# A fused attention and mixture kernel: which queue loads the second batch, and when the later batches' maxima are read

## The chip, the cores and the metric

One core of one Trainium2 chip runs the whole program. The metric is the device time of one launch in microseconds (us), as the median of several runs. The engines are PE (TensorE, matrix products), ACT (ScalarE), DVE (VectorE), POOL (GpSimd) and SP (SyncE, which here issues DMA transfers and nothing else). POOL issues DMA transfers too, between its own arithmetic. Each engine works through a list of its own in order, so an instruction that waits holds up those behind it in that list.

## The reference

```python
q_n, k_n = rmsnorm(q, g_q), rmsnorm(k, g_k)           # x / sqrt(mean(x*x) + 1e-6) * g, over D = 64
scores = (1 / sqrt(64)) * q_n @ k_n.T                 # B, H, S, D = 4, 12, 448, 64
attn = softmax(scores)                                # max taken off, sum + 1e-9
x = (attn @ v).transpose(0, 2, 1, 3).reshape(1792, 768)
h = x @ w_in                                          # 768 x 2048
x = (h * sigmoid(1.702 * h)) @ w_out                  # 2048 x 768
h = x @ w2_in
out = (maximum(h, 0) + alpha * minimum(h, 0)) @ w2_out
```

All inputs are float32, and the output is float32 of 1792 x 768. The weights of the two layers come as 64-bit words.

## The kernel before, in words

**Tiling.** The twelve heads of a batch are handled in NP = 6 pairs, so there are 24 pairs, numbered P = 0 to 23, six to each of the four batches b. A pair's queries and keys are one `qk` tile of four DMA transfers (`load_qk`, L354 to L357, a ring of three tiles), its values one `vr` tile of three (`load_v`, L370, L372, L373). `normalize` (L385) takes one or two pairs: ACT squares (L397), DVE sums them into `ss` (L399), and POOL works out the inverse roots `rs`: L400 and L403, then three rounds of the four operations L407 to L410, 14 in all. Pairs 0 and 1 have a `normalize` each (on 14 columns); later calls take two pairs (28 columns).

**Stages.** Batch 0 runs first, in float32 (`first_pairs`): DVE multiplies with the roots (`qn`, L434), PE transposes, scores, row maxima (`nm`, L506), exponentials on ACT. Beside it the first layer's weights are made: SP loads raw words (L222, into rings of R1I = 5 and R1O = 4 places), ACT and DVE turn them into float32 (`from_words`, L147, L163, L164), DVE takes row maxima (L244), and ACT and DVE split them in two float16 halves (`split_rows`, L179). Batches 1 to 3 run in split float16, with `hl` and `ph` transposed by DMA (L456, L601, L606), while PE interleaves the first layer of the batch before. The second layer follows, from about 600 us on, and keeps PE busy to the end.

**The maxima of v.** A batch's values are scaled by a power of two below their largest magnitude, `av[:, b]`. Batch 0's maximum is taken pair by pair (L446). For batches 1 to 3 `v_scale(b)` (L304) reads the whole batch once more: VN = 8 loads of 128 x 336 float32 into `vst` (L310, two buffers, on POOL's queue), each followed by a DVE reduction into a column of `vcol` (L311), and `v_scales` (L297) then takes the maximum over columns and partitions. `av[:, b]` is first needed when the batch's first pair splits its values into `vs` (`split`, L139 and L140, called at L460).

**What sets the order.** The program is written in one order, and the framework's scheduler, which works with its own estimate of time, writes each engine's list from it. `tc.issue_after(ins)` lets what is in its block be queued on `ins`'s engine only behind `ins`; it binds nothing on other engines. `v_scale(1)` stands in a block behind the last load of the first layer's first weight (L1212, an SP instruction), `v_scale(2)` and `v_scale(3)` behind `moved[P]`, the transposing DMA of a pair's `hl` (L456, L705, an SP instruction too), where P is a batch's next to last pair. The loads L310 are POOL instructions. `load_qk` and `load_v` go to SP's queue for batch 0 and to POOL's for batches 1 to 3 (L353, L369).

Of the kernel before, what the change touches and what calls it, by code (L numbers as in the profile page):

```python
# [56 lines left out]
def attention_moe_kernel(  # L57
# [246 lines left out]
    def v_scale(b):  # L304
        flat = v[b].rearrange("h s d -> (h s d)").rearrange("(p n) -> p n", p=128)
        n = flat.shape[1] // VN
        col = small.tile([128, VN], F32, tag="vcol", name="vcol")
        for i in range(VN):
            t = raw_p.tile([128, n], F32, tag="vst", name="vst")
            nc.gpsimd.dma_start(out=t, in_=flat[:, i * n:(i + 1) * n])  # L310
            nc.vector.tensor_reduce(out=col[:, i:i + 1], in_=t, op=ALU.max, axis=AX, apply_absolute_value=True)  # L311
        v_scales(b, col)

# [28 lines left out]
    def some_rows(src, b, p, first, step=1):  # L342

        return src[b, 2 * p:2 * p + 2, first:first + 64 * step:step].rearrange("h s d -> s h d")

    def load_qk(P):

        if P >= B * NP:
            return
        b, p = divmod(P, NP)  # L350
        qk = raw_p.tile([128, 2, NT2, D], F32, tag="qk", name="qk", bufs=QKB)
        places = qk.rearrange("p h c d -> p h (c d)")
        queue = nc.gpsimd if b else nc.sync  # L353
        queue.dma_start(out=places[:, :, 0:3 * D], in_=main_rows(k, b, p))  # L354
        queue.dma_start(out=places[:, :, 4 * D:], in_=main_rows(q, b, p))
        queue.dma_start(out=qk[0:64, :, 3], in_=some_rows(k, b, p, ST))
        queue.dma_start(out=qk[64:128, :, 3], in_=some_rows(q, b, p, ST))  # L357
        raws[P] = qk

    def load_v(P):  # L360
        if P >= B * NP:
            return
        b, p = divmod(P, NP)
        if b:
            vr = raw_p.tile([128, 2, NV, D], F32, tag="vr", name="vr")
        else:
            firsts[P] = first_tiles(P)
            vr = firsts[P][1]
        queue = nc.gpsimd if b else nc.sync  # L369
        queue.dma_start(out=vr.rearrange("p h c d -> p h (c d)")[:, :, 0:3 * D], in_=main_rows(v, b, p))  # L370
        h = 0 if b else 64
        queue.dma_start(out=vr[h:h + 64, :, 3], in_=some_rows(v, b, p, ST))  # L372
        queue.dma_start(out=vr[64 - h:128 - h, :, 3], in_=some_rows(v, b, p, 0, 3))  # L373
        rawv[P] = vr
# [2 lines left out]
    roots = {}  # L377
    v0 = const.tile([128, NP], F32, name="v0")
    moved = {}

    def side(P):

# [2 lines left out]
    def normalize(*Ps):  # L385

        Ps = [P for P in Ps if P < B * NP]
        if not Ps:
            return
        n = NT2  # L390
        w = 2 * n * len(Ps)
        ss = small.tile([128, 4 * NT2], F32, tag="ss", name="ss")[:, 0:w]
        for t, P in enumerate(Ps):
            flat = raws[P].rearrange("p h c d -> p (h c) d")
            for i in range(2):
                sq = att_p.tile([128, n, D], F32, tag="sq", name="sq", bufs=SQB)
                nc.scalar.activation(out=sq, in_=flat[:, i * n:(i + 1) * n], func=AF.Square, scale=2.0 ** -13)  # L397
                o = (2 * t + i) * n
                nc.vector.tensor_reduce(out=ss[:, o:o + n], in_=sq, op=ALU.add, axis=AX)  # L399
        nc.gpsimd.tensor_scalar(out=ss, in0=ss, scalar1=1e-6 * 2.0 ** -20, scalar2=None, op0=ALU.add)  # L400
        rs = small.tile([128, 4 * NT2], F32, tag="rs", name="rs")[:, 0:w]
        tn = small.tile([128, 4 * NT2], F32, tag="tn", name="tn")[:, 0:w]
        nc.gpsimd.tensor_scalar(  # L403
            out=rs.bitcast(I32), in0=ss.bitcast(I32), scalar1=-0.5, scalar2=RSQRT_SEED, op0=ALU.mult, op1=ALU.add
        )
        for _ in range(3):
            nc.gpsimd.tensor_tensor(out=tn, in0=rs, in1=rs, op=ALU.mult)  # L407
            nc.gpsimd.tensor_tensor(out=tn, in0=tn, in1=ss, op=ALU.mult)
            nc.gpsimd.tensor_scalar(out=tn, in0=tn, scalar1=-0.5, scalar2=1.5, op0=ALU.mult, op1=ALU.add)
            nc.gpsimd.tensor_tensor(out=rs, in0=tn, in1=rs, op=ALU.mult)  # L410
        for t, P in enumerate(Ps):
            eng = side(P)
            ks = raws[P][:, :, 0:4]
            flat = raws[P].rearrange("p h c d -> p (h c) d")
            root = rs[:, 2 * n * t:2 * n * (t + 1)]
            if P < NP:
                roots[P] = root
                continue
            eng.tensor_tensor(out=ks, in0=ks, in1=gs.unsqueeze(1).to_broadcast([128, 2, 4, D]), op=ALU.mult)
            eng.tensor_tensor(out=flat, in0=flat, in1=root.unsqueeze(2).to_broadcast([128, 2 * n, D]), op=ALU.mult)  # L420
# [274 lines left out]
    def other_batches():  # L695
        for i, _ in enumerate(attention(list(range(4 * NP, NU)))):
            P, r = divmod(4 * NP + i, 4)
            if P < B * NP:
# [3 lines left out]
                if r == NORM_AT and P % 2 == 0:  # L702
                    normalize(P + 2, P + 3)
                if r == 2 and P % NP == NP - 2 and P // NP + 1 < B:
                    with tc.issue_after(moved[P].ins):  # L705
                        v_scale(P // NP + 1)
                if r == 3:
                    load_qk(P + 1 + QKB)
# [565 lines left out]
```

## Time and profile before

| | |
|---|---|
| runs | 1175.09, 1175.65, 1180.21 us; median 1175.65 |
| the profiled execution | 1178.25 us, of which the span of the trace is 1176.5 |
| PE busy | 1064.7 us (91% of the span) |
| DVE busy | 818.7 us (70%) |
| ACT busy | 671.9 us (57%) |
| POOL busy | 178.1 us (15%) |
| transfers moved | 158.05 MB, of them 17.11 by POOL's queue |

The shares are means over stages that differ, so the table by stretch, which gives each engine's busy time in a piece of the span, comes first. In a timeline a row gives the start, the duration, the engine, the line and operation, output and input; the bracket at its end is the idle time of the engine just before it and what ended that. An issue of a DMA takes an engine's time, and the transfer goes on after it; "landing" is the time from issue to the data's arrival. The engine name SPq stands for SP's sequencer. "PEclk" is the mean clock granted to TensorE, where 1.00 is 2.4 GHz.

### The profile page before, as it was taken

Reading aid. Unit: us, or ns where it says so; the run is one execution under the profiler, and the core shown is the slowest. Engines: PE = TensorE matmul, PEld = TensorE weight load, DVE = VectorE, ACT = ScalarE, POOL = GpSimd, SP = SyncE. Lnnn points to the kernel's source line nnn. Section 1 sums busy time; section 2 is a strip of 40 time slices with the busy share of each in tenths; the row PEclk is TensorE's granted clock in tenths of the full one; section 3 lists DMA queues with packets and bytes.
Section 4 is the critical chain, followed back from the end, with each engine's and each line's share of the span. In section 5 each row is a group of like instructions: output and inputs, shape, how many; then the busy total and the mean of one; then the engine's idle time right before and its main releaser. Section 6 shows DMA issues by size and latency. Waiting matters only on the chain.

```text
span 1176.5 us, 18337 instructions
## 1 busy us (share of the span) xinstructions
PE 1064.7 (91%) x6755; PEld 586.5 (50%) x6755; DVE 818.7 (70%) x1445; ACT 671.9 (57%) x1348; POOL 178.1 (15%) x350
## 2 busy tenths in 40 slices
PE   1468898679889999999999999999999999999998
PEld 0234456554344445555455455544444477666664
DVE  5979899887776876567651958499987322978351
ACT  3658676687776786668842645266545323645220
POOL 5331002667333323201000000000000000000000
PEclk9679799879999999999999999999999999999999
DMA  8863544477898677566563911465633323353011
GB/s 266 245 209 91 162 139 115 93 146 144 158 182 122 134 139 131 118 117 122 94 132 94 328 45 52 143 221 188 215 110 114 136 76 120 99 177 101 32 33 29
DMA packets 233130, 158.05 MB, mean 134 GB/s; under 512 B 166704, under 2 KB 211888, under 8 KB 233040
## 3 DMA queue, kind: packets, MB, share of 16 engines
q1 hardware_dynamic: 226128, 139.77, 46.0%
q0 software_dynamic: 6912, 17.11, 6.0%
q8 instruction: 53, 0.87, 0.3%
q14 instruction: 37, 0.30, 0.1%
HBM read 92.22 MB, written 25.69 MB: 100 GB/s over the span
## 4 chain that ended last, share of the span: by engine, by line
PE 38%; DVE 21%; DMA 14%; ACT 13%; issue 8%; POOL 5%; SPq 1%; ACTq 0%; DVEq 0%; POOLq 0%
PE op L1058 16%; PE h L898 10%; PE yp L796 5%; ACT pr L525 4%; DMA qk<-in_q_dram 4%; DVE nm L506 3%; PE hp L773 3%; PE hp L726 2%; DVE ph L594 2%; ACT ph L567 2%; DMA g<-in_moe_w_out_dram 2%; DMA yr<-y_dram 1%; DMA t<-hl 1%; DMA w2raw<-in_moe_w_in_dram 1%; DMA g<-in_moe_w_in_dram 1%
## 5 line engine op out<-in xcount | busy, mean ns | idle before, releaser
L796 PE MATMUL yp<-g,w1o 128*128 128x448 f16 x1152 | 226.1, 354 | 0.0
L898 PE MATMUL h<-x,w2i 128*128 128x512 f16 (+1 forms) x1152 | 218.9, 353 | 3.7 <-DVE pos L904 2.9
L773 PE MATMUL hp<-x,w1i 128*128 128x448 f16 x864 | 170.1, 354 | 1.4 <-DVE t L782 1.4
L898 PEld LDWEIGHTS <-w2i 128*128 128x128 f16 x1152 | 112.5, 98 | 109.2 <-issue 4.5
L796 PEld LDWEIGHTS <-w1o 128*128 128x128 f16 x1152 | 109.7, 98 | 108.1 <-issue 8.7
L773 PEld LDWEIGHTS <-w1i 128*128 128x128 f16 x864 | 82.4, 98 | 84.1 <-issue 10.1
L594 DVE SCALAR_TENSOR_TENSOR ph<-pr,sm,ph 128x448 f16<-128x448 f32 x126 | 88.4, 731 | 20.6 <-ACT ph L567 20.5
L506 DVE TENSOR_REDUCE nm<-sp 128x2 f32<-128x896 f32 x96 | 92.3, 961 | 3.0 <-PE sp L501 3.0
L525 ACT ACTIVATE pr<-sp,nm,c_s 128x448 f32<-128x448 f32 x126 | 89.9, 717 | 2.0 <-DVE ph L594 0.6
L903 ACT ACTIVATE pos<-h,sign 128x512 f32<-128x512 f32 (+1 forms) x64 | 40.1, 628 | 86.2 <-PE h L898 80.4
L567 ACT ACTIVATE ph<-pr,sm 128x448 f16<-128x448 f32 x126 | 77.9, 660 | 18.0 <-DVE sm L564 17.9
L1058 PEld LDWEIGHTS <-even 128*128 128x128 f16 x672 | 65.6, 98 | 43.5
L904 DVE SCALAR_TENSOR_TENSOR pos<-h,slope,pos 128x512 f32<-128x512 f32 (+1 forms) x64 | 43.4, 680 | 59.2 <-ACT pos L903 59.2
L726 PE MATMUL hp<-x,w1i 128*128 128x256 f16 (+1 forms) x576 | 66.5, 279 | 11.3 <-DVE t L738 7.8
L501 PE MATMUL sp<-t 64*128 64x448 f16 (+1 forms) x432 | 54.8, 361 | 17.5 <-ACT pr L525 16.3
L726 PEld LDWEIGHTS <-w1i 128*128 128x128 f16 x576 | 56.4, 105 | 22.5 <-issue 17.5
L1058 PEld LDWEIGHTS <-odd 128*128 128x128 f16 x504 | 49.3, 98 | 32.6
L1058 PE MATMUL op<-w2lo,even 128*128 128x384 f16 x384 | 63.4, 326 | 0.0
L140 DVE SCALAR_TENSOR_TENSOR g<-t,ratio_w1o,g 128x448 f16<-128x448 f32 x64 | 44.7, 705 | 18.4 <-ACT g L139 18.0
L622 PE MATMUL xp<-pt,vs 128*64 128x256 f16 (+1 forms) x792 | 47.2, 265 | 8.8 <-DMA pt<-ph 6.7
L139 ACT ACTIVATE g<-t,ratio_w1o 128x448 f16<-128x448 f32 x64 | 42.0, 664 | 20.8 <-DVE t L782 18.6
L508 ACT ACTIVATE nm<-nm,c_s 128x2 f32<-128x2 f32 x72 | 20.8, 289 | 54.7 <-DVE nm L506 54.5
(236 smaller groups left out, 1644.8 us busy)
## 6 DMA issues: line engine op xcount, KB each, us to landing
g<-in_moe_w_in_dram SPq DMA_DIRECT2D x24, 512.0 KB, 5.7
g<-in_moe_w_out_dram SPq DMA_DIRECT2D x32, 384.0 KB, 4.1
w2raw<-in_moe_w_in_dram SPq DMA_DIRECT2D x24, 512.0 KB, 5.6
w2raw<-in_moe_w_out_dram SPq DMA_DIRECT2D x16, 768.0 KB, 6.4
g_dram<-pos SPq DMA_DIRECT2D x48, 256.0 KB, 2.0
gp<-g_dram SPq DMA_DIRECT2D x8, 1024.0 KB, 7.3
odd<-g_dram SPq DMA_DIRECT2D x6, 1024.0 KB, 5.4
y_dram<-y SPq DMA_DIRECT2D x24, 224.0 KB, 3.4
```

Of the source, the lines that this page charges most:

```text
L140: nc.vector.scalar_tensor_tensor(out=dst[1], in0=src, scalar=scale, in1=dst[0], op0=ALU.mult, op1=ALU.subtract)
L501: nc.tensor.matmul(out=sp[:, j, 0:S] if n == 2 else sp[ds, 0, 0:S], lhsT=qt[ds] if n == 2 else qt[ds, 64:128], rhs=kt[ds, 0:S], start=(i = ...
L506: nc.vector.tensor_reduce(out=nm[:, 0:n], in_=sp[:, 0:n, 0:S], op=ALU.max, axis=AX, negate=True)
L525: nc.scalar.activation(out=pr[i], in_=sp[:, i, 0:S], func=AF.Exp, bias=nm[:, i:i + 1], scale=c_s if u >= 4 * NP else 1.0, accum_out=sm[:, ...
L567: nc.scalar.activation(out=ph[:, i, 0:S], in_=pr[i], func=AF.Copy, scale=sm[:, i:i + 1])
L594: nc.vector.scalar_tensor_tensor(out=ph[:, i, S:2 * S], in0=pr[i], scalar=sm[:, i:i + 1], in1=ph[:, i, 0:S], op0=ALU.mult, op1=ALU.subtract)
L622: nc.tensor.matmul(out=xp[64 * j:64 * j + 64, t:t + n], lhsT=vs[ks, j, c], rhs=pt[ks, 7 * j + kc, 0:n] if b else pt[ks, kc, o:o + n], star ...
L726: nc.tensor.matmul(out=ps, lhsT=w1i[:, kk, e, m * 128:(m + 1) * 128], rhs=xs[0, kk][:, f, cols], start=(i == 0), stop=(i == 3 * KD - 1))
L773: nc.tensor.matmul(out=ps, lhsT=w1i[:, kk, e, m * 128:(m + 1) * 128], rhs=x[:, f], start=(n == 0), stop=(n == 3 * KD - 1))
L796: nc.tensor.matmul(out=ps, lhsT=w1o[:, m, e, j * 128:(j + 1) * 128], rhs=g[:, m, f], start=(n == 0), stop=(n == 3 * KF - 1))
L898: nc.tensor.matmul(out=ps, lhsT=w2i[:, kk, e, m * 128:(m + 1) * 128], rhs=x2[kk][:, f], start=(c == 0), stop=(c == 3 * KD - 1))
L1058: nc.tensor.matmul(out=ps, lhsT=ops[:, o, m, f], rhs=rhs[:, e], start=(c == 0), stop=(c == 3 * KH - 1))
```

## The change

Three edits:

- `v_scale(1)` loads its eight `vst` tiles on SP's queue; those of batches 2 and 3 stay on POOL's.
- A new function `loader(P)` picks the queue of a pair's loads: SP for pairs 0 to 7, POOL from pair 8 on. So the loads of pairs 6 and 7 (batch 1's first two, 14 transfers) change to SP. With the eight `vst` loads that is 22 transfers from POOL to SP.
- `normalize` keeps its last POOL instruction, the last L410, in `rooted[Ps[0]]`, and the blocks of `v_scale(2)` and `v_scale(3)` stand behind `rooted[P + 2]` in place of `moved[P]`. That is a POOL instruction, as the loads are: the roots of pairs 12 and 13 for batch 2, of pairs 18 and 19 for batch 3.

```diff
-            nc.gpsimd.dma_start(out=t, in_=flat[:, i * n:(i + 1) * n])
+            (nc.sync if b == 1 else nc.gpsimd).dma_start(out=t, in_=flat[:, i * n:(i + 1) * n])
...
+    def loader(P):
+
+        return nc.gpsimd if P >= NP + 2 else nc.sync
+
...
-        queue = nc.gpsimd if b else nc.sync
+        queue = loader(P)
...
+    rooted = {}
...
-            nc.gpsimd.tensor_tensor(out=rs, in0=tn, in1=rs, op=ALU.mult)
+            rooted[Ps[0]] = nc.gpsimd.tensor_tensor(out=rs, in0=tn, in1=rs, op=ALU.mult)
...
-                    with tc.issue_after(moved[P].ins):
+                    with tc.issue_after(rooted[P + 2].ins):
                         v_scale(P // NP + 1)
```

The line `queue = ...` occurs twice, in `load_qk` and in `load_v`. Line numbers behind L347 grow by 4 in the changed kernel, behind L369 too, and by 5 behind L383: L354 becomes L358, L370 becomes L374, L410 becomes L415. L310 and L222 keep theirs. No instruction is added or left out; the lists of PE, ACT and DVE hold the same instructions in another order.

**POOL at the start.** The first pairs' roots before, with the first loads of `vst` and of `vr` ahead of them (the `vr` rows are those of pairs 6 and 7):

```order
L370 DMA vr<-in_v_dram 128x2x192
L372 DMA vr<-in_v_dram 64x2x64
L373 DMA vr<-in_v_dram 64x2x64
L310 DMA vst<-in_v_dram 128x336 x2
L400 TENSOR_SCALAR ss<-ss 128x14
L403 TENSOR_SCALAR rs<-ss 128x14
L407 TENSOR_TENSOR tn<-rs 128x14
L408 TENSOR_TENSOR tn<-tn,ss 128x14
L409 TENSOR_SCALAR tn<-tn 128x14
L400 TENSOR_SCALAR ss<-ss 128x14
L410 TENSOR_TENSOR rs<-tn,rs 128x14
L310 DMA vst<-in_v_dram 128x336
```

and now:

```order
masks.py:199 AFFINE_SELECT ident<-ident 128x128
L405 TENSOR_SCALAR ss<-ss 128x14
L408 TENSOR_SCALAR rs<-ss 128x14
L412 TENSOR_TENSOR tn<-rs 128x14
L413 TENSOR_TENSOR tn<-tn,ss 128x14
L414 TENSOR_SCALAR tn<-tn 128x14
L415 TENSOR_TENSOR rs<-tn,rs 128x14
L412 TENSOR_TENSOR tn<-rs 128x14
L413 TENSOR_TENSOR tn<-tn,ss 128x14
L414 TENSOR_SCALAR tn<-tn 128x14
L415 TENSOR_TENSOR rs<-tn,rs 128x14
L412 TENSOR_TENSOR tn<-rs 128x14
```

The first pair's 14 operations now follow one another, and neither `vr` nor `vst` loads stand before them; the second pair's come behind.

**SP around the transfer of a maximum through DRAM** (L127 writes the column `am` out as `line`, L128 reads it back as `row`; `g_143` is the place of the raw weight words). Before:

```order
L357 DMA qk<-in_q_dram 64x2x64
L222 DMA g_143<-in_moe_w_in_dram 128x1024 x5
L127 DMA line_7326<-am 128x1
L128 DMA row<-line_7326 128x128
L222 DMA g_143<-in_moe_w_in_dram 128x1024 x5
L222 DMA g_143<-in_moe_w_out_dram 128x4x192 x31
```

and now:

```order
L222 DMA g_143<-in_moe_w_in_dram 128x1024 x2
L358 DMA qk<-in_k_dram 128x2x192
L359 DMA qk<-in_q_dram 128x2x192
L222 DMA g_143<-in_moe_w_in_dram 128x1024
L360 DMA qk<-in_k_dram 64x2x64
L361 DMA qk<-in_q_dram 64x2x64
L222 DMA g_143<-in_moe_w_in_dram 128x1024 x3
L310 DMA vst<-in_v_dram 128x336 x4
L222 DMA g_143<-in_moe_w_out_dram 128x4x192
L310 DMA vst<-in_v_dram 128x336
L222 DMA g_143<-in_moe_w_out_dram 128x4x192
L310 DMA vst<-in_v_dram 128x336 x3
```

Before, the pair of rows L127, L128 is followed by w_in loads and 31 loads of w_out. Now the rest of the w_in loads has a `qk` tile of pair 6 or 7 between, and the eight `vst` loads of batch 1 stand around the first two loads of w_out.

**POOL behind the roots of pairs 12 and 13.** Before:

```order
L410 TENSOR_TENSOR rs<-tn,rs 128x28
L370 DMA vr<-in_v_dram 128x2x192
L372 DMA vr<-in_v_dram 64x2x64
L373 DMA vr<-in_v_dram 64x2x64
L354 DMA qk<-in_k_dram 128x2x192
L355 DMA qk<-in_q_dram 128x2x192
L356 DMA qk<-in_k_dram 64x2x64
L357 DMA qk<-in_q_dram 64x2x64
L400 TENSOR_SCALAR ss<-ss 128x28
L403 TENSOR_SCALAR rs<-ss 128x28
```

and now:

```order
L415 TENSOR_TENSOR rs<-tn,rs 128x28
L310 DMA vst<-in_v_dram 128x336 x3
L374 DMA vr<-in_v_dram 128x2x192
L376 DMA vr<-in_v_dram 64x2x64
L377 DMA vr<-in_v_dram 64x2x64
L310 DMA vst<-in_v_dram 128x336
L358 DMA qk<-in_k_dram 128x2x192
L359 DMA qk<-in_q_dram 128x2x192
L360 DMA qk<-in_k_dram 64x2x64
L361 DMA qk<-in_q_dram 64x2x64
L310 DMA vst<-in_v_dram 128x336 x3
L405 TENSOR_SCALAR ss<-ss 128x28
```

Behind the last root operation there now stand seven of batch 2's eight `vst` loads among the loads of a later pair's `vr` and `qk`, ahead of the next roots. Batch 3's eight stand in the same way behind the roots of pairs 18 and 19.

## Rows read from the trace of the kernel before

**Rows 1.** Table by stretch; its columns are in the first line of the fence.

```profile
core 0: us, PE busy (x) PEld busy (x) DVE busy (x) ACT busy (x) POOL busy (x), PEclk, DMA share, GB/s
0.00:30.00 30.00, 6.33 (x18) 2.97 (x19) 16.85 (x37) 10.30 (x17) 15.84 (x45) 1.00 0.85 267
30.00:62.00 32.00, 17.19 (x79) 9.45 (x78) 32.00 (x66) 21.91 (x43) 10.62 (x24) 0.68 0.83 255
62.00:77.00 15.00, 11.65 (x59) 5.51 (x58) 8.32 (x20) 7.00 (x17) 6.71 (x17) 0.77 0.60 142
77.00:120.00 43.00, 31.79 (x192) 18.25 (x194) 42.88 (x77) 33.73 (x69) 8.28 (x14) 0.84 0.44 136
...
180.00:215.00 35.00, 29.18 (x292) 24.93 (x293) 31.80 (x72) 21.19 (x43) 10.33 (x24) 1.00 0.28 74
...
285.00:345.00 60.00, 51.91 (x403) 26.48 (x401) 46.04 (x77) 44.56 (x109) 25.73 (x49) 1.00 0.86 164
...
435.00:600.00 165.00, 165.00 (x1148) 83.58 (x1143) 106.68 (x183) 117.71 (x273) 26.08 (x55) 1.00 0.61 117
600.00:1176.50 576.50, 564.74 (x3217) 308.12 (x3215) 353.69 (x556) 247.55 (x382) 0.00 (x0) 1.00 0.38 122
sum 1176.50, PE 1064.71 PEld 586.47 DVE 818.66 ACT 671.92 POOL 178.09; mean PE 88.73 PEld 48.87 DVE 68.22 ACT 55.99 POOL 14.84
```

**Rows 2.** Timeline of POOL, 10 to 17 us: start, duration, what it does, idle before.

```profile
10.81 0.26 POOL L400 TENSOR_SCALAR ss<-ss 128x14 f32<-128x14 f32 x1 [3.61 <-DVE ss L399]
...
12.04 0.21 POOL L409 TENSOR_SCALAR tn<-tn 128x14 f32<-128x14 f32 x1
16.00 0.26 POOL L400 TENSOR_SCALAR ss<-ss 128x14 f32<-128x14 f32 x1 [3.75 <-DVE ss L399]
```

**Rows 3.** Timeline of DVE, first 62 us.

```profile
22.36 1.09 DVE L434 TENSOR_TENSOR qn<-qk,rs 128x896 f32<-128x896 f32 x1 [2.04 <-POOL rs L410]
```

**Rows 4.** Timeline of SP, issues only.

```profile
5.45 0.61 SPq L373 DMA_DIRECT2D w1o<-in_v_dram  x1
...
62.68 0.33 SPq L127 DMA_DIRECT2D line<-am  x1
71.24 0.33 SPq L128 DMA_DIRECT2D row<-line  x1
71.74 9.80 SPq L222 DMA_DIRECT2D g<-in_moe_w_in_dram  x5
94.37 90.11 SPq L222 DMA_DIRECT2D g<-in_moe_w_out_dram  x31
```

**Rows 5.** Timeline of DVE, 62 to 130 us.

```profile
72.39 0.50 DVE L311 TENSOR_REDUCE vcol<-vst 128x1 f32<-128x336 f32 x1 [3.57 <-DMA vst<-in_v_dram]
...
76.33 0.28 DVE L133 TENSOR_REDUCE a<-row 128x1 f32<-128x128 f32 x1 [3.11 <-DMA row<-line]
```

**Rows 6.** Chain of waits, 285 to 345 us: start, duration, what.

```profile
306.64 0.73 POOL qk L354
...
308.69 6.37 DMA qk<-in_q_dram
```

**Rows 7.** Tile view of `vst`: line, engine, count, ns min/median/max, first to last start.

```profile
L310 POOL DMA_DIRECT2D vst<-in_v_dram x24: 536/556/792, 6.1 to 111.3; - x24
L311 DVE TENSOR_REDUCE vcol<-vst x24: 481/492/503, 15.8 to 114.6; 128x1 f32<-128x336 f32 x24
...
DMA to landing us min/median/max: 2.4/4.0/7.4
```

**Rows 8.** Timeline of DVE once more, around 99 us.

```profile
98.86 0.49 DVE L311 TENSOR_REDUCE vcol<-vst 128x1 f32<-128x336 f32 x1
99.27 0.14 DVE L104 TENSOR_SCALAR rm_w1i<-rm_w1i 128x1 f32<-128x1 f32 x1
```

**Rows 9.** Timeline of POOL around 295 us.

```profile
295.19 0.24 POOL L410 TENSOR_TENSOR rs<-tn,rs 128x28 f32<-128x28 f32 x1
```

**Rows 10.** Timeline of DVE, 283 to 345 us.

```profile
340.17 0.75 DVE L140 SCALAR_TENSOR_TENSOR vs<-vr,av,vs 128x512 f16<-128x512 f32 x1 [0.50 <-ACT vs L139]
```

More of the change, by code (lines that the diff above doesn't have):

```diff
@@ L368, in load_v @@
             vr = firsts[P][1]
-        queue = nc.gpsimd if b else nc.sync
+        queue = loader(P)
         queue.dma_start(out=vr.rearrange("p h c d -> p h (c d)")[:, :, 0:3 * D], in_=main_rows(v, b, p))
```

## The prediction

> **What bounds the kernel now.** The table by stretch comes first [rows 1]. From 435 to 600 us PE is busy for 165.00 of 165.00 us, and from 600 to the end for 564.74 of 576.50. Over the span PE is idle 1176.50 - 1064.71 = 111.8 us, 11.8 of them behind 600 and none from 435 to 600, so 100.0 us of idle PE lie ahead of 435. Only from these can a change of order take time; what it adds behind 435 shows only if it makes PE wait.
>
> In the early part DVE is the bound: 32.00 of 32.00 us from 30 to 62, 42.88 of 43.00 from 77 to 120, and still 31.80 of 35.00 from 180 to 215 [rows 1]. A DVE instruction taken out there moves what stands behind it forward by its own time. From 285 to 345 none of the engines is full (PE 51.91, DVE 46.04 of 60.00), and the DMA share is 0.86 [rows 1]: there the chain of waits goes through POOL's issue of a pair's `qk` and a landing of 6.37 us [rows 6].
>
> Three places stand out in the timelines. POOL begins the first pair's roots at 10.81, gets as far as L409 at 12.04, and goes on only behind the second pair's L400, which starts at 16.00 after 3.75 us of idling for `ss` [rows 2]. DVE starts the first `qn` (L434) at 22.36, 2.04 us idle for those roots [rows 3]. And DVE idles 3.57 us for a `vst` load and 3.11 us for `row`, while SP, having issued `line` at 62.68, sends `row` only at 71.24 [rows 4, 5].
>
> **The change part by part.** The sum stands against the profiled execution of 1178.25 us (span 1176.5, and 1.75 around it), which is 2.60 above the median of the runs, 1175.65; each difference is then taken from the median.
>
> A. *Sixteen reductions leave the first 215 us.* All 24 loads of `vst` go out between 6.1 and 111.3 us, and their reductions run from 15.8 to 114.6 [rows 7]. Now only batch 1's eight stay there; those of batches 2 and 3 come behind the roots of pairs 12 and 18. A reduction starts at 98.86 and the next instruction at 99.27, so it takes 0.41 us of DVE's line [rows 8]: 16 x 0.41 = 6.6. The two maxima over columns that follow later are left out of the sum. DVE is the bound there, so I take all: **-6.6** (bounds 0 and -6.6).
>
> B. *The first pair's roots run without a break.* Four operations, 10.81 to 12.04, are 0.31 each [rows 2], so 14 take 4.3 and end at 15.1, and `qn` could start 22.36 - 15.1 = 7.2 earlier. But DVE did other needed work in between, and only the 2.04 it idled are sure [rows 3]. **-2.0** (bounds 0 and -7.2).
>
> C. *The wait for `row`.* SP's place for L127 and L128 among the w_in loads stays, so their 71.24 - 62.68 = 8.6 stay too [rows 4]. The 3.57 for `vst` go, but without other work DVE would wait as long for `row`. DVE's new list has five `qn` ahead of the reduction of `row`, where four were; one is 1.09 long [rows 3]. **-1.1** (bounds 0 and -3.1, the whole second wait [rows 5]).
>
> D. *SP gets 22 issues more, POOL 22 fewer.* POOL's are no price: it is busy 15.84 of 30.00 at the start and 8.28 of 43.00 from 77 to 120 [rows 1]. On SP four `qk` issues now stand between w_in loads behind `row`, 0.61 each [rows 4]: 2.4. The eight `vst` loads stand around the first two w_out loads. They have two buffers, so they go in four rounds of issue, landing and reduction, 0.56 + 4.0 + 0.49 = 5.05 each [rows 7], 20.2 together; SP had 94.37 - (71.74 + 9.80) = 12.8 with nothing to issue in that place [rows 4]. What is over, 7.4, is the upper bound, the lower 0. I take the four issues, **+2.4**.
>
> What stands in SP's line costs more than its issue here: 31 w_out loads are drawn out over 90.11 us, 2.9 a load [rows 4], since each waits for a free place. The Trainium skill (DMA: Bandwidth & Descriptors, section "Issuing engines are not separate DMA queues") says that transfers started by any engine run on the same 16 DMA engines and interleave, so that the choice of issuer only saves issue time, usually small. By that D would be about 0 and the total 2.4 lower, 1169.3; the rows on waiting issues speak against so small a view of it.
>
> E. *Batch 2's loads now lie around 295 to 325 us.* Their block follows the last L410 of pairs 12 and 13, at 295.19 [rows 9]. `av` of batch 2 is first needed by pair 12's `vs`, whose DVE part runs at 340.17 [rows 10], 45 us later, so the maximum itself is in time. What can be late is what is queued behind the loads. On POOL four of them stand ahead of the next `qk` loads, which before went out at 306.64 [rows 6]: two rounds, 10.1, fit in the 306.64 - 295.43 = 11.2 between. On DVE the eight reductions are new, 8 x 0.41 = 3.3, in a stretch where DVE is busy 46.04 of 60.00 and holds up the chain. If every round trip lay open, E would be 4 x 5.05 = 20.2. Since the rounds fit the gap on POOL, I take the reductions alone, **+3.3** (bounds 0 and +20.2).
>
> F. *Batch 3's loads* follow the roots of pairs 18 and 19, in the stretch with PE full and DVE busy 106.68 of 165.00 [rows 1]: 58.3 us of DVE idle cover 3.3 of reductions. **0** (upper bound one round, 5.05, if that cover fails at the one place).
>
> Sum: -6.6 - 2.0 - 1.1 + 2.4 + 3.3 + 0 = **-4.0**, so 1174.25 for an execution like the profiled one, and **1171.7** for the median.
>
> **The rivals.** About 0.5%, 5.9 us, is what a measurement of this kernel can tell from no change: faster is below 1169.8, slower above 1181.5.
>
> R1, *the late loads are hidden and the start gives more.* B is taken halfway to its bound (-4.6), D and E are 0: -6.6 - 4.6 - 1.1 = -12.3, 1163.4. For it: the gap on POOL and the 45 us before the maximum is needed; and at the start the DMA share is 0.85 [rows 1], with 22 transfers fewer crowding the first landings. Against: DVE's work in the break was needed anyway.
>
> R2, *DVE's freed time turns into waits for words.* The reductions leave, but the weights still arrive as they did, with a DMA share of 0.83 from 30 to 62 [rows 1], and DVE waits for them: 0, 1175.7. Against: DVE showed no idle time at all in that stretch.
>
> R3, *slower: the round trips of batch 2's loads lie open.* The place is DVE's line around 295 to 325: a reduction waits there for its landing with the row maxima and `hl` behind it, and POOL's next load for that reduction, with `qk` behind it. Price: 20.2 in place of 3.3, so -7.3 + 20.2 = +12.9, 1188.6. It decides from E = 13.2 on (-7.3 + 13.2 = 5.9). For it: landings of 6.37 are on the chain there [rows 6], and DMA is at 0.86. Against: POOL's gap of 11.2.
>
> R4, *it doesn't do what it says*: the framework could order the loads early again. POOL's new list shows them behind the roots, so 1175.7 is nearly excluded.
>
> R5, *POOL's loads land late because DVE is busy.* With every landing at the longest seen, 7.4, a round is 0.56 + 7.4 + 0.49 = 8.45 [rows 7], four are 33.8: -7.3 + 33.8 = +26.5, 1202.2. Against: DVE was full from 30 to 62 with such loads in flight, and of 24 none took over 7.4, half of them 4.0 or less. The Trainium skill (SBUF — State Buffer, section "SBUF: two separate sides") has such a rule: a transfer issued by GpSimd is starved of descriptors while VectorE holds the port they share, in some of its modes. The trace does not show it at work.
>
> **How the numbers follow.** Forecast 0.45, own range 1166.5 to 1175.5 (D and E each some 4 lower or higher); R1 0.22; R2 0.13; R3 0.15; R4 0.02; R5 0.03. Faster: R1 and four ninths of the forecast's case, 0.22 + 0.20 = 0.42. Slower: R3 and R5, 0.18. Within 0.5%: the rest of the forecast's case 0.25, R2 and R4, 0.40. The low end of the range is R1 with B and C at their bounds, -6.6 - 7.2 - 3.1 = -16.9, 1158.8, so 1159. The high end, 1183, is E at 14.7, short of R3's full price; it leaves out R5, two thirds of R3 and the tails.
>
> **What would show it.** Eight `vcol` reductions before 215 us in place of 24. First `qn` near 15 to 20 in place of 22.36 (B). SP's `row` still some 8.6 behind `line` (C). The first w_out load at 94 or later by no more than 7 (D). The last L415 of pairs 12 and 13 near 295.19 - 7.3 = 288, and pair 12's `vs` near 336 (E). DVE waiting for `vst` for under 5 us in all between 285 and 345; over 13 would be R3. PE full from about 431. The prediction is wrong if that last point does not move, or moves by over 12.

## The result, and the profile after

The changed kernel takes 1182.99 us in the median of 22 runs (1176.80 to 1190.82), the kernel before 1175.47 in its 22 (1169.29 to 1180.21). The ratio is 1.0070, 95% interval [1.0054, 1.0087]: slower by some 8 us. Forecast were 1171.7, and 0.18 for slower. The time lies just inside the range that was given (1159 to 1183), on the wrong side of no change. The profiled execution took 1184.22 us, its span is 1182.4, 5.9 more than before.

The table by stretch of the changed kernel, with the columns of [rows 1]:

```profile
core 0: us, PE busy (x) PEld busy (x) DVE busy (x) ACT busy (x) POOL busy (x), PEclk, DMA share, GB/s
0.00:30.00 30.00, 12.77 (x37) 6.00 (x37) 18.56 (x38) 13.42 (x27) 7.79 (x34) 1.00 0.72 227
30.00:62.00 32.00, 16.42 (x69) 8.19 (x69) 29.09 (x62) 20.34 (x39) 10.16 (x28) 1.00 0.86 252
77.00:120.00 43.00, 33.37 (x206) 17.60 (x204) 40.84 (x83) 33.85 (x73) 0.00 (x0) 0.87 0.49 141
285.00:345.00 60.00, 48.01 (x343) 23.61 (x342) 46.66 (x85) 42.04 (x104) 28.19 (x53) 0.91 0.99 183
...
435.00:600.00 165.00, 164.18 (x1144) 83.29 (x1139) 107.48 (x184) 117.66 (x273) 28.26 (x58) 1.00 0.62 120
600.00:1182.40 582.40, 571.40 (x3246) 311.67 (x3244) 356.12 (x561) 250.45 (x389) 0.00 (x0) 1.00 0.38 122
```

DVE is no longer full from 30 to 62 and from 77 to 120, as was meant. From 285 to 345 the DMA share has gone from 0.86 to 0.99 and PE's busy time from 51.91 to 48.01. Behind 435 PE is nearly as full as before (164.18 of 165.00 in place of 165.00).

What the start gained is there. POOL's timeline, the first pair's roots, against [rows 2]:

```profile
9.36 0.26 POOL L405 TENSOR_SCALAR ss<-ss 128x14 f32<-128x14 f32 x1 [8.06 <-DVE ss L404]
...
13.25 0.22 POOL L415 TENSOR_TENSOR rs<-tn,rs 128x14 f32<-128x14 f32 x1
```

They run from 9.36 to 13.47 without a break, and the first `qn` starts at 13.50 in place of 22.36 [rows 3]; the second row is the reduction of `row`, 6.2 us earlier than in [rows 5] with a wait for it as long as before, 3.40 in place of 3.11 (DVE's timeline):

```profile
13.50 1.09 DVE L439 TENSOR_TENSOR qn<-qk,rs 128x896 f32<-128x896 f32 x1 [0.39 <-POOL rs L415]
...
70.12 0.29 DVE L133 TENSOR_REDUCE a<-row 128x1 f32<-128x128 f32 x1 [3.40 <-DMA row<-line]
```

SP's timeline, against [rows 4]: `row` goes out 7.3 us behind `line` (8.6 before), and the first w_out load at 91.19 (94.37 before), though four `vst` loads stand ahead of it. Counted from `line`, which itself comes 5.3 earlier, that load is 33.8 behind, where it was 31.7.

```profile
57.40 0.34 SPq L127 DMA_DIRECT2D line<-am  x1
64.67 0.33 SPq L128 DMA_DIRECT2D row<-line  x1
...
78.49 10.27 SPq L310 DMA_DIRECT2D vst<-in_v_dram  x4
91.19 0.38 SPq L222 DMA_DIRECT2D g<-in_moe_w_out_dram  x1
```

The tile view of `vst`, against [rows 7]: eight loads on SP between 78 and 100 us, sixteen on POOL from 292.8 on; the longest landing is 9.3 in place of 7.4.

```profile
L311 DVE TENSOR_REDUCE vcol<-vst x24: 470/495/504, 87.1 to 430.6; 128x1 f32<-128x336 f32 x24
L310 POOL DMA_DIRECT2D vst<-in_v_dram x16: 537/567/627, 292.8 to 427.5; - x16
L310 SPq DMA_DIRECT2D vst<-in_v_dram x8: 327/375/717, 78.5 to 100.0; - x8
...
DMA to landing us min/median/max: 2.2/3.7/9.3
```

POOL's timeline around 295, against [rows 9]: the last root operation of pairs 12 and 13 comes at 292.13, only 3.1 us earlier than before.

```profile
262.71 0.78 POOL L374 DMA_DIRECT2D vr<-in_v_dram  x1 [3.31 <-DVE vs L140]
...
292.13 0.24 POOL L415 TENSOR_TENSOR rs<-tn,rs 128x28 f32<-128x28 f32 x1
292.76 1.23 POOL L310 DMA_DIRECT2D vst<-in_v_dram  x2 [0.38 <-issue]
```

The chain of waits from 285 to 365 us: it still goes through the landing of a `qk` load, now 9.06 in place of 6.37 [rows 6], and twice in these rows through a transposing DMA.

```profile
297.84 4.04 DMA t<-hl
...
306.52 9.06 DMA qk<-in_q_dram
...
333.54 5.24 DMA t<-hl
```

DVE's timeline: of the eight reductions of batch 2 one waits for its load, for 1.00 us; pair 12's `vs` is at 343.82, 3.7 later than in [rows 10].

```profile
321.77 0.50 DVE L311 TENSOR_REDUCE vcol<-vst 128x1 f32<-128x336 f32 x1 [1.00 <-DMA vst<-in_v_dram]
...
343.82 0.75 DVE L140 SCALAR_TENSOR_TENSOR vs<-vr,av,vs 128x512 f16<-128x512 f32 x1
```

Batch 3's loads do not lie where step F of the prediction had them. In the kernel before, the roots of pairs 18 and 19 end at 402.73, ahead of the stretch from 435 on in which PE is full, and the changed kernel issues batch 3's loads from 405.56 to 428.0 (POOL's timelines, before and after):

```profile
402.49 0.24 POOL L410 TENSOR_TENSOR rs<-tn,rs 128x28 f32<-128x28 f32 x1
```

```profile
405.56 1.19 POOL L310 DMA_DIRECT2D vst<-in_v_dram  x2
```

PE's last wait ahead of 600 us ends at 421.96 in the kernel before (2.26 long) and at 445.72 here (0.73 long; PE's timelines).

Three marks cut the span into four stages: SP's first transpose of `hl`, DVE's part of `vs` of pair 10, and that of pair 18. In the kernel before, and then in the changed one (SP's and DVE's timelines):

```profile
213.68 2.63 SPq L456 DMA_TRANSPOSE t<-hl  x1
302.11 0.73 DVE L140 SCALAR_TENSOR_TENSOR vs<-vr,av,vs 128x512 f16<-128x512 f32 x1
481.09 0.75 DVE L140 SCALAR_TENSOR_TENSOR vs<-vr,av,vs 128x512 f16<-128x512 f32 x1 [1.23 <-ACT vs L139]
```

```profile
206.42 9.65 SPq L461 DMA_TRANSPOSE t<-hl  x2
299.76 0.73 DVE L140 SCALAR_TENSOR_TENSOR vs<-vr,av,vs 128x512 f16<-128x512 f32 x1
485.51 0.75 DVE L140 SCALAR_TENSOR_TENSOR vs<-vr,av,vs 128x512 f16<-128x512 f32 x1 [1.23 <-ACT vs L139]
```

| stage | before | after | difference |
|---|---|---|---|
| 1: start to first `hl` transpose | 213.7 | 206.4 | -7.3 |
| 2: to pair 10's `vs` | 88.4 | 93.3 | +4.9 |
| 3: to pair 18's `vs` | 179.0 | 185.8 | +6.8 |
| 4: to the end | 695.4 | 696.9 | +1.5 |

So in these two executions the early gain came, more than half of it was given back before the first late load was issued (292.76), and the stretch with the late loads lost as much again.

### The profile page after: what moved, and what is told of

The parts are those of the page before. It is cut to its first block, busy times and chain, and to the rows that moved or that the text cites. A ratio compares the mean times of both kernels' runs of the same rounds, so it can differ in the third digit from the quotient of the medians.

```text
span 1182.4 us, 18333 instructions
## 1 busy us (share of the span) xinstructions
PE 1074.1 (91%) x6755; PEld 587.0 (50%) x6755; DVE 823.5 (70%) x1445; ACT 672.8 (57%) x1348; POOL 161.4 (14%) x328
## 4 chain that ended last, share of the span: by engine, by line
PE 37%; DVE 23%; DMA 15%; ACT 13%; issue 7%; POOL 3%; SPq 2%; ACTq 0%; DVEq 0%; POOLq 0%
PE op L1063 16%; PE h L903 7%; PE yp L801 6%; ACT pr L530 4%; DMA qk<-in_q_dram 3%; DVE nm L511 3%; PE hp L778 3%; DVE ph L599 3%; PE hp L731 3%; DMA t<-hl 2%; DMA yr<-y_dram 2%; ACT ph L572 2%; PE xp L627 2%; DVE g L140 1%; DMA g<-in_moe_w_in_dram 1%
## 5 line engine op out<-in xcount | busy, mean ns | idle before, releaser
L801 PE MATMUL yp<-g,w1o 128*128 128x448 f16 x1152 | 229.5, 357 | 2.4 <-DVE t L743 1.9
L599 DVE SCALAR_TENSOR_TENSOR ph<-pr,sm,ph 128x448 f16<-128x448 f32 x126 | 91.2, 750 | 17.4 <-ACT ph L572 17.4
L506 PE MATMUL sp<-t 64*128 64x448 f16 (+1 forms) x432 | 57.2, 369 | 21.9 <-ACT pr L530 15.3
L627 PE MATMUL xp<-pt,vs 128*64 128x256 f16 (+1 forms) x792 | 49.7, 272 | 13.0 <-DMA pt<-ph 8.9
L627 PEld LDWEIGHTS <-vs 128*64 128x64 f16 x792 | 38.9, 114 | 29.6 <-issue 16.7
```

Source lines behind the costliest of these rows:

```text
L506: nc.tensor.matmul(out=sp[:, j, 0:S] if n == 2 else sp[ds, 0, 0:S], lhsT=qt[ds] if n == 2 else qt[ds, 64:128], rhs=kt[ds, 0:S], start=(i = ...
L599: nc.vector.scalar_tensor_tensor(out=ph[:, i, S:2 * S], in0=pr[i], scalar=sm[:, i:i + 1], in1=ph[:, i, 0:S], op0=ALU.mult, op1=ALU.subtract)
L627: nc.tensor.matmul(out=xp[64 * j:64 * j + 64, t:t + n], lhsT=vs[ks, j, c], rhs=pt[ks, 7 * j + kc, 0:n] if b else pt[ks, kc, o:o + n], star ...
L801: nc.tensor.matmul(out=ps, lhsT=w1o[:, m, e, j * 128:(j + 1) * 128], rhs=g[:, m, f], start=(n == 0), stop=(n == 3 * KF - 1))
```

## The experiments

In the pieces of code below, `...` stands for what is left out of a line. Three theories stood at first. **L**: the late loads of batches 2 and 3 cost the time. **Q**: the change of queues does. **O**: the scheduler's lists come out in another order in a stretch that the diff does not name, and that order does. Ratios are to the kernel before, with 95% intervals.

**The two halves of the change.**

```diff
# q_only: the changed kernel with
-                    with tc.issue_after(rooted[P + 2].ins):
+                    with tc.issue_after(moved[P].ins):
# r_only: the changed kernel with
-            (nc.sync if b == 1 else nc.gpsimd).dma_start(out=t, ...)
+            nc.gpsimd.dma_start(out=t, ...)
-        return nc.gpsimd if P >= NP + 2 else nc.sync
+        return nc.gpsimd if P >= NP else nc.sync
```

> Only the queues change: batch 1's vst loads and the loads of pairs 6 and 7 go to SP, the later batches' loads stay unbound as before. Theory L (the late loads of batches 2 and 3 cost the time, in the stretch from 290 to 435 us): within 4 us of the kernel before, 1171 to 1179, since no load is late. Theory Q (the queue change costs it, through SP's longer line): 5 us or more slower than before, 1181 or more. Theory O (the lists of POOL, SP and DVE come out in another order from 215 us on, and that order costs it, whatever caused it): 3 to 5 slower, if this list is like the changed kernel's there.

> Only the late loads: batches 2 and 3 behind the roots, queues as before. Theory L: slower than before by 3 to 10, 1179 to 1186, with PE reaching 435 us later by as much, since 16 reductions fewer early give at most 6.6 and the late loads cost more. Theory Q: no slower than before, 1169 to 1175. Theory O: 3 to 5 slower only if its list from 215 on is like the changed kernel's.

Measured: q_only 1169.14 (0.9934 [0.9909, 0.9959]), r_only 1183.67 (1.0058 [1.0034, 1.0083]). Theory Q falls: the queue part alone is faster than the kernel before, by 6.6 us in the median, and so than the changed one. The late loads alone are slower by about as much as the whole change. In q_only all sixteen loads of batches 2 and 3 go out from 102 to 144 us (tile view of `vst`):

```profile
L310 POOL DMA_DIRECT2D vst<-in_v_dram x16: 536/538/773, 102.4 to 143.8; - x16
L310 SPq DMA_DIRECT2D vst<-in_v_dram x8: 328/375/552, 79.3 to 100.8; - x8
```

**Without the sixteen loads and reductions.**

```diff
     def v_scale(b):
+        if b > 1:
+            v_scales(b, vcols[1])
+            return
```

> The changed kernel without the 16 loads and reductions of batches 2 and 3, which take batch 1's maximum in place of their own. Theory L: 8 to 14 faster than the changed kernel, 1169 to 1175, since the whole of what is late is gone and the early gain stays. Theory Q: still slower than before, 1179 to 1183. Theory O: 3 to 5 of the loss stays, 1177 to 1180.

> The kernel before without the 16 loads and reductions of batches 2 and 3, which take batch 1's maximum in place of their own; queues as before. It prices the sixteen early reductions: 6.6 if DVE's line is the bound there (1168 to 1170), 0 to 2 if other waits take their place (1174 to 1176). Theory L has after_none within 3 of this run, theory Q has after_none 5 or more above it.

Measured: after_none 1176.99 (0.9999 [0.9971, 1.0026]), before_none 1174.69 (0.9989 [0.9962, 1.0015]). The late block costs 0.7% with either choice of queues: after_none to the changed kernel 0.0071, before_none to r_only 0.0069. Yet after_none stands 2 above the range that theory L gave it, and its lists leave the changed kernel's from 112 us on, so a part of the difference may be order. And the sixteen early reductions cost next to nothing: taking them from the kernel before saves 1.3 us by the ratio, at most 4.5 by the interval, where step A had 6.6. Stranger, after_none does strictly less than q_only: it lacks the sixteen loads and reductions, its lists differ from 102 us on otherwise in order alone, and it is 0.65% above it.

**The two halves of the queue part.** l_only takes `loader`, v1_only `nc.sync` for batch 1's `vst`, each put into the kernel before.

> Of the queue part only the loads of pairs 6 and 7 go to SP; all vst loads stay on GpSimd and unbound as before. Theory P (the gain of the queue part, 6.6, comes from GpSimd's line at the start: pairs 6 and 7's v loads stood ahead of the first roots): most of the gain, 1169 to 1172, with the first qn some 5 us earlier than before. Theory V (it comes from the vst loads that no longer stand between the roots): no gain, 1174 to 1178, first qn near 22 as before.

> Of the queue part only batch 1's eight vst loads go to SP, behind the last load of the first weight; the rest as before. Theory V: most of the gain of the queue part, 1168 to 1172, first qn some 5 us or more earlier. Theory P: no gain, 1174 to 1178. If neither of the two halves gains, the gain hangs on both together or on the order of the lists behind 215 us.

Measured: 1174.00 (0.9974 [0.9953, 0.9994]) and 1175.95 (0.9981 [0.9957, 1.0005]). Neither of P and V holds alone: each half gives 0.2 to 0.3% of the whole part's 0.5 to 0.7, v1_only's interval takes in no change, and the two are not told apart. The first `qn` starts at 23.29 in l_only, later than before, and at 16.03 in v1_only (DVE's timelines). So it is the `vst` loads between the roots that held up the first `qn`, as V has it; but l_only gains no less without that, so the time of the first `qn` is not what the gain hangs on.

**Loads or reductions?** Two theories of the late block, T (transfers) and W (DVE's line).

```diff
# after_nored
-            nc.vector.tensor_reduce(...)
+            if b == 1:
+                nc.vector.tensor_reduce(...)
# after_noload, for b > 1
-            t = raw_p.tile([128, n], F32, tag="vst", name="vst")
-            nc.gpsimd.dma_start(out=t, ...)
+            t = w1i[:, 0, 0, 0:2 * n].bitcast(F32)
```

> The changed kernel with the late loads of batches 2 and 3, but without their 16 reductions; their maxima are batch 1's. Theory T (the transfers cost it: 1.38 MB more for each batch in a stretch whose DMA share is 0.86, and longer landings of qk): stays near the changed kernel, 1180 to 1184. Theory W (DVE's reductions and their waits for landings, in order ahead of other work, cost it): falls to the kernel without both, 1175 to 1179.

> The changed kernel without the late loads; the 16 reductions stay, at the same place in DVE's list (behind the scaling of pair 12 and of pair 18), over data that is long in SBUF, and the maxima are batch 1's. Theory T: falls to the kernel without both, 1175 to 1179. Theory W: the work alone is 3.3 a batch and no landing is waited for, so between, 1178 to 1182.

In after_noload `rooted` is also the last scaling with the roots (L433, on DVE) in place of the last root operation, so the reductions stay late: batch 2's eight stand in one piece from 298.8 to 302.2.

Measured: after_nored 1181.33 (1.0037 [1.0010, 1.0064]), after_noload 1175.86 (0.9987 [0.9969, 1.0004]). Sixteen late reductions without loads cost nothing; late loads without reductions do, by about half of the changed kernel's 0.7%. Whether the reductions add the rest when they come with their loads is not told apart: the intervals overlap. From 290 to 345 us, the row of the table by stretch of after_noload and then of the changed kernel (columns as above):

```profile
290.00:345.00 55.00, 48.65 (x339) 23.96 (x338) 41.05 (x80) 40.95 (x99) 18.55 (x40) 0.94 0.76 162
```

```profile
290.00:345.00 55.00, 43.01 (x302) 20.88 (x299) 42.52 (x82) 39.40 (x96) 23.19 (x47) 0.91 0.98 186
```

Without the loads the DMA share is 0.76 in place of 0.98, and PE is busy for 5.6 us more. But the share does not tell the kernels apart. The same row of after_half (half of each late load, below) and of q_only (no late loads at all):

```profile
290.00:345.00 55.00, 48.99 (x365) 24.02 (x363) 43.22 (x84) 42.23 (x105) 24.89 (x49) 0.97 1.01 188
```

```profile
290.00:345.00 55.00, 49.03 (x354) 23.55 (x353) 41.56 (x76) 43.39 (x107) 19.29 (x35) 0.96 0.93 174
```

At 1.01 and 0.93 PE is as busy there as at 0.76. The landings of `qk` tell more: the longest from 290 to 345 us is 9.1 in the changed kernel, 9.4 in r_only and 11.3 in after_sp (tile views of `qk`), and 4.9 to 7.2 in all other kernels. Among these are after_nored (5.9) and after_vr10b (6.1), whose late loads are full too, so the landings do not tell all.

**Fewer bytes, another issuer, other places.** after_half loads 168 of the 336 columns of each late tile, after_t8 8 of them; after_sp puts the late loads on `nc.sync` behind `moved[P]`; late3_only keeps `rooted[P + 2]` for batch 3 alone; after_r6 puts both behind `rooted[NP]`, the roots of pairs 6 and 7.

> The changed kernel with loads of half the width for batches 2 and 3 (their maxima are taken over half of the values): as many loads and reductions, half the bytes. Theory T by bytes: half of what the late loads cost, so 1178 to 1181. If the number of round trips and issues sets it: as the changed kernel, 1181 to 1185.

> The changed kernel with late loads of 8 columns in place of 336 (maxima of batches 2 and 3 over those): as many loads, issues and reductions, 1/42 of the bytes, SP's list word for word that of the changed kernel. Theory T by bytes: ratio to before 0.998 to 1.001, as with no loads at all. If issues and round trips or the order of the lists cost it: 1.004 to 1.007, as the changed kernel.

> The changed kernel with the late loads of batches 2 and 3 on SP's line, behind the transposing DMA of the pair where the block stands. If the transfers themselves cost it, whoever issues them: 1180 to 1186, as the changed kernel. If GpSimd's line costs it (loads ahead of qk issues and of roots): 3 us or more faster than the changed kernel, 1175 to 1180. If SP's transposes wait behind loads that wait for a buffer: 1187 or more.

> The changed kernel, but only batch 3's loads are late; batch 2's are unbound and early, as in the kernel with the queue part alone (1169). If batch 2's late loads cost it: 1169 to 1173. If batch 3's cost as much: 1174 to 1178. If any late block brings the unfavourable list from 110 to 300 us: 1177 or more.

> The changed kernel with the loads of batches 2 and 3 queued behind the roots of pairs 6 and 7, near 200 us, where the DMA share was 0.28 to 0.32, in place of behind those of pairs 12 and 18. Theory T: free of the cost from 300 us on; that stretch (pair 10's vs to pair 18's vs) falls from 185.8 to 173 to 180, and the ratio to 0.995 to 1.001, unless GpSimd's line, where these loads now stand between qk loads, gives it back from 210 to 300.

| kernel | late loads | median | ratio | interval |
|---|---|---|---|---|
| after_noload | none | 1175.86 | 0.9987 | [0.9969, 1.0004] |
| after_t8 | 16, 8 columns | 1177.02 | 1.0024 | [0.9999, 1.0049] |
| after_half | 16, 168 columns | 1180.54 | 1.0007 | [0.9986, 1.0029] |
| changed kernel | 16, 336 columns | 1182.99 | 1.0070 | [1.0054, 1.0087] |
| after_sp | 16, 336 columns, on SP | 1186.67 | 1.0061 | [1.0033, 1.0089] |
| late3_only | 8, 336 columns | 1180.73 | 1.0028 | [1.0003, 1.0053] |
| after_r6 | 16, 336 columns, 197 to 259 us | 1178.76 | 1.0014 | [0.9993, 1.0035] |

With as many loads and issues, half the bytes or a 42nd of them lie below the full ones, with intervals that end at 1.0029 and 1.0049 where the changed kernel's begins at 1.0054; so most of the cost comes with the full width. Half and a 42nd are not told apart, and after_t8's 1.0024 lies between the ranges of its two theories. That the bytes themselves cost it is argued: the lists of POOL, SP, DVE and ACT in after_half and after_t8 are the changed kernel's up to 311 and 304 us, and differ in order behind that. (Ratios compare better than medians here, since each goes to runs of the kernel before on its own chip.) Who issues these loads makes no difference clear of noise, 1.0061 from SP and 1.0070 from POOL, though in after_sp they begin at 281 us, in another order of the lists. The Trainium skill (DMA: Bandwidth & Descriptors, section "Issuing engines are not separate DMA queues") says that DMA transfers run on the same 16 DMA engines whichever engine started them; these two runs agree. late3_only lies between, so batch 3's loads are not free either; against q_only, from which it differs by the place of batch 3's loads and the order of the lists from 124 us on, it is 0.75 to 0.94% slower. Its time lies in the range of its last branch, an unfavourable order, which is not excluded.

The same sixteen loads near 200 to 260 us leave stage 3 at 174.4, as theory T has it (tile view of after_r6), but stage 2 takes 99.9 there, as the expectation's last clause feared:

```profile
L310 POOL DMA_DIRECT2D vst<-in_v_dram x16: 554/584/632, 197.0 to 258.6; - x16
```

**Order.** q_again is q_only once more; q_t84 and q_t168 load a quarter and half of the width early.

> The queue part alone once more, the same kernel as q_only: ratio 0.991 to 0.996 if that gain is the kernel's own; 0.998 or more if it was that session's.

> The queue part alone with a quarter of the width in the early loads of batches 2 and 3: strictly less work than q_only, in another order of the lists from 110 us on. If the sixteen reductions were a price on DVE's line (step A): 0.988 to 0.993, some 3 us below q_only. If the order of the lists decides: anywhere from 0.993 to 1.001, above q_only although it does less.

> As q_t84 with half the width, in yet another order of the lists. Step A: 0.990 to 0.995. Order: anywhere from 0.993 to 1.001, and not between q_only and q_t84.

Measured: q_again 1168.52 (0.9953 [0.9933, 0.9974]), q_t84 1171.03 (0.9976 [0.9949, 1.0003]), q_t168 1171.55 (0.9981 [0.9959, 1.0003]). The gain of q_only is its own, not that of one session. The two that do less are not below it, as step A would have them; both medians lie above it, though the intervals overlap. Two moves on POOL's list tested a single place:

```diff
# before_vr10: load_v(10) behind the roots of pairs 10 and 11
+                    if P == 8:
+                        with tc.issue_after(rooted[P + 2].ins):
+                            load_v(P + 2)
# after_vr10b: load_v(10) behind the POOL part of pair 10's hl; load_v(11) stands after it, unbound
+        if P == 10:
+            with tc.issue_after(low_.ins):
+                load_v(P)
```

> The kernel before with one move in GpSimd's list alone: pair 10's three v loads stand behind the roots of pairs 10 and 11 in place of ahead of them; the lists of all other engines stay word for word. Theory O (from 215 to 300 us it matters where the v loads, which wait for a buffer, stand among the roots): the wait of 1.26 and the three issues of 2.0 no longer delay the roots, so 2 to 4 faster than before, 1171 to 1174. Without theory O: within 1 us of before.

> The changed kernel with pair 10's v loads on GpSimd behind pair 10's hl operation in place of ahead of it; all lists up to there stay. Theory O, by this one place: the stretch from the first transpose of hl to pair 10's vs, 93.3 us in the changed kernel, falls by 2 to 5, and the ratio to before by 0.002 to 0.004, to 1.003 to 1.005. If this place is not what the stretch hangs on: 93 within 2 us, and 1.006 to 1.008.

Measured: before_vr10 1178.46 (1.0010 [0.9985, 1.0035]), after_vr10b 1189.64 (1.0084 [1.0054, 1.0114]). Theory O by this one place fails in both: before_vr10 is within 1 us of before, and in after_vr10b the `hl` operation indeed stands ahead of the load (POOL's timeline), but stage 2 takes 92.1, no different from 93.3:

```profile
261.84 1.88 POOL L459 TENSOR_TENSOR hl<-qk,hl 128x896 f16<-128x896 f32 x1 [3.16 <-ACT hl L458]
263.66 0.78 POOL L374 DMA_DIRECT2D vr<-in_v_dram  x1
```

Stages 1 to 3 of the traces, by the same marks:

```
               stage 1  stage 2  stage 3
before           213.7     88.4    179.0
before_none      205.8     89.1    177.3
q_only           209.7     84.6    175.1
q_again          210.4     85.6    172.3
after_none       210.0     88.3    180.5
after_nored      209.2     89.2    187.4
after_noload     206.2     98.2    173.6
after_t8         208.2     92.6    183.5
after_half       204.6     94.5    179.6
after            206.4     93.3    185.8
after_sp         204.8     96.1    188.3
r_only           208.5     91.4    188.7
```

Each is one execution, and those lay between 3.6 below and 9.8 above the median of their kernel, so a single difference of a few us says little: the lists of POOL, SP, DVE and ACT in after, after_noload, after_t8 and after_half are the same up to 292 us, and their stage 1 takes 204.6 to 208.2. Over the lines: stage 3 is 185.8 to 188.7 in the four with full-width loads late, 172.3 to 180.5 in the six with none late. The kernels that are not listed agree: 193.0 in after_vr10b and 185.5 in late3_only, with batch 3's loads alone, against 171.5 to 177.6 in six without full-width loads in that stage. Stage 2 is 91.4 to 98.2 in the six that have the reductions late, 84.6 to 89.2 in the other six. (In after_noload, 98.2, it holds 3.4 of late reductions, most of which elsewhere come behind the mark.) In the first six it is long whether full loads follow or none do, so it may hang on the lists. Kernels that are not listed speak against reading much into stage 2: v1_only and before_vr10, with nothing late, have 96.2 and 91.2 there.

## Why the prediction was wrong

**The start was right in sum by the traces (A to D), and partly by luck.** Steps A to D gave -6.6 - 2.0 - 1.1 + 2.4 = -7.3, and stage 1 is 7.3 shorter. That they agree so closely is luck: kernels with the same lists up to there have a stage 1 of 204.6 to 208.2. Single steps are not all borne out. B's mark moved more than its bound (first `qn` 8.9 earlier, bound 7.2), 1.5 of it because the roots themselves begin earlier. C's wait for `row` stayed. D's issue of `qk` loads shows at most as the 2.1 by which the first w_out load comes later behind `line`.

**Step A failed as the text put it, "DVE is the bound there, so I take all".** A gain in stage 1 was carried into the sum as if it lasted to the end. Over whole runs, taking the sixteen reductions from the kernel before gained 1.3 us in place of 6.6 (at most 4.5). Within stage 1 the traces do not refute A: before_none's is 7.9 shorter than before's. Where the rest goes is not shown. In the changed kernel's trace 4.9 of the 7.3 were gone at 300 us; before_none's one trace keeps its gain, but it is an execution 3.6 below its kernel's median, beside one of the kernel before that is 2.6 above. With the changed kernel's queues, leaving the sixteen out cost time: after_none lies 0.65% above q_only. DVE's full stretch ends at 215, and what follows from 215 to 300 is a stage with other limits, whose lists were changed too. The prediction compared lists at three places and never there. What costs the 5 us there is not settled: the one place tried, the `vr` loads on POOL that wait 3.31 us ahead of `hl`, is not it.

**Steps E and F were the terms of the wrong size.** E charged batch 2's loads with 3.3 of DVE's reductions, and found that the rounds fit POOL's gap. Both views were right and did not price them: the reductions alone cost nothing (after_noload), DVE waited 1.00 us for batch 2's loads and 3.3 for batch 3's, the next `qk` loads were issued at 304.50, no later than in [rows 6], and moving the issue away from POOL saves nothing clear of noise (after_sp). F took 0 because PE is full where batch 3's loads lie. That was misread: they go out ahead of 435, where PE still waits. What the runs showed in place of 3.3 and 0: the late block as a whole costs 0.69 to 0.71%, 8 us for E and F together, it needs the loads (after_noload) and most of it their full width (after_half, after_t8), and it falls in stage 3, 6.8 longer in the trace. E left out that the loads are transfers beside those on the chain, where the landing of a `qk` load grew from 6.37 to 9.06. By which path full-width loads cost what they do is not shown; the mean DMA share does not say, and the order of the lists behind 293 us changed with every variant.

**The rivals.** R3 had the sign right, and its total was too high (1188.6), since it charged round trips on DVE's line, which did not lie open. R4 did not occur: the loads went out late. Nor did R5: a longest landing of 9.3 and a median of 3.7, and loads issued from SP cost as much as from POOL. R1's case for the start, a B near its bound, is what the first `qn` did, and R2's waits for words came in part (DVE waits 2.65 us for ACT's half of the conversion at 50.23); neither looked past 215.

**The numbers behind the chances.** From 1166.5 to 1175.5 the part below 1169.8 is 3.3 of 9.0, so 0.17 of the forecast's 0.45 and not four ninths of it, 0.20. "PE full from about 431" took 435, the border of a row of the table, for the point from which PE is full; by its last wait that is 422 before, and it moved later, to 446, not 4 earlier.

In sum, by the ratios in a row (before, before_none, after_none, after): step A -1.3 in place of -6.6, B to D near 0 without the early loads (+0.0010 of ratio), the late block +8.3. These add up to the 8.2 us of the result by construction. In another order the parts are others: from before to q_only -5.5 to -7.8, from there to the changed kernel +14 to +16. So the price of a step depends on what else is changed.

What stays open: why the queue part gains 0.5 to 0.7% with sixteen full early loads in place (q_only, q_again) and nothing without them (after_none). Beside the work the order of the lists from 102 us on differs, and q_t84 and q_t168, with other orders, lie between; but no run held the work and the queues fixed and changed the order alone, save at single places that showed nothing.

The version that beats both kernels is q_only: the queue changes without the later binding, 1169.14 and 1168.52 on two chips.

## What to carry to other kernels

Before moving loads to a later place, look at the landings on the chain there: loads whose own consumer waits 1 us can still cost 8. The mean DMA share did not tell here, 1.01 with half the bytes and no loss clear of noise, 0.98 with all and a loss. And see where the loads will lie in time before taking them as hidden. A gain on the engine that bounds an early stage is worth what the next stage passes on; price it over the whole run, by the variant that leaves the work out. Where a scheduler makes the lists, a change can reorder a stretch it never names, so compare all of every list, and test a change in halves: here one half was a gain and the other a loss.

## What the runs showed of the hardware

TensorE's granted clock fell where PE had been starved for a while. The changed kernel from 320 to 340 us, then the kernel before (table by stretch, columns as above):

```profile
320.00:330.00 10.00, 4.83 (x46) 2.56 (x44) 9.00 (x17) 7.98 (x19) 8.47 (x19) 1.00 0.93 192
330.00:340.00 10.00, 8.19 (x34) 3.65 (x34) 8.01 (x23) 7.26 (x18) 0.38 (x1) 0.66 0.99 173
```

```profile
320.00:330.00 10.00, 9.39 (x69) 4.62 (x68) 8.81 (x13) 6.92 (x18) 5.60 (x13) 1.00 0.68 140
330.00:340.00 10.00, 8.34 (x65) 4.14 (x66) 6.89 (x14) 8.14 (x21) 2.15 (x4) 1.00 0.94 173
```

PE is busy 4.83 of 10 us from 320 to 330, and from 330 to 340 the granted clock is 0.66 in the mean, between its two levels of 1.2 and 2.4 GHz. Before, PE is busy 9.39 of the first ten, and the clock stays at 1.00. Six matmuls of one form in either kernel (PE's timelines; first the changed one, with the waits ahead):

```profile
325.23 1.39 PE L627 MATMUL xp<-pt,vs 128*64 128x256 f16 x22 [2.47 <-DMA pt<-ph]
331.81 1.33 PE L506 MATMUL sp<-t 64*64 64x448 f16 x6 [4.52 <-ACT pr L530]
```

```profile
333.08 0.76 PE L501 MATMUL sp<-t 64*64 64x448 f16 x6
```

They take 1.33 in place of 0.76 us. So waits of PE, here 2.47 for a transposing DMA and 4.52 for ACT, were paid a second time, in PE's speed after them; no run took the two apart.
